# A causal convolution in front of a spectral mixer: x stored two rows to a partition, the convolution on the four quarters of the array

## The chip, the cores and the metric

The kernel runs on one core of one Trainium2 chip. The metric is device time in microseconds (us) of one execution. Three timed runs of the kernel before gave 175.7, 175.7 and 176.12 us, median 175.7 us. The core's engines have these names in the rows: PE is TensorE's matmul stream and PEld its weight loads, DVE is VectorE, ACT is ScalarE, POOL is GpSimd (here it issues the input transfers) and SP is the queue of the output transfers.

## The reference

Two blocks, one after the other, on `x` of shape (8, 3264, 192):

```python
# block 1: softmax over 7 taps for each of 8 heads, causal convolution along the rows
w = softmax(weight, axis=-1)                       # (8 heads, 7 taps)
x_pad = concatenate([zeros((B, 6, D)), x], axis=1)
u = einsum('hk,bskhg->bshg', w, x_pad[:, s + k])   # 24 columns to a head
# block 2: 64 lowest modes of the row axis are mixed over the 192 columns
X = rfft(u, axis=1)[:, :64]
Y = X @ (w_r + 1j * w_i)                           # one 192 x 192 matrix for each mode
u = u + irfft(Y, n=3264, axis=1)
out = u + relu(u @ w_ch)
```

The input x and the output are 20 MB each in float32, the mode matrices 19 MB.

## The kernel before, in words

**Stages.** The kernel goes through four stages that overlap. It loads x with a cast to bf16 on the way and convolves it; it takes the forward transform as matmuls against a table (`ftab`); it mixes the modes with matrices that stream in behind x; and it forms `u`, the clamp and the sum in a second stage that writes the output while it computes.

**Units.** Each of the four pairs of batches (`q`) is cut into units of one or two blocks of 256 rows. There are 14 units, numbered from 0 by the loop over `units`: the first pair has five small ones (`UNITS0`, four of one block and one of two), the other three have three units of two blocks each (`UNITS`). Units run from the last rows of a pair to the first. The last unit of a pair also takes the 96 rows that are left over (`rest`): units 4, 7, 10 and 13. Both batches of a pair and both halves of a batch lie beside each other in the columns of an operand, so a unit of two blocks has 8 row blocks of 24 columns for a head (192 columns) and one with rest has 10 (240 columns).

**Loading.** `load_unit` issues on POOL, for each block of 128 rows, one transfer that puts one row of x into one partition; `load_rest` brings the rows left over. Then POOL issues the mode matrices (`load_w`): sixteen groups of four modes, eight into the parts of `ct` that are still unused, four into `arena`, and the last four into `arena` again, each as soon as `mix` has read the group that lay there.

**The convolution.** `conv_pass` takes two of the eight heads. The weights of a product are 64 columns of a band matrix (`bd3`), every second column of it, so that the result comes out by parities: even rows of 256 in one half of the bank, odd rows in the other. Every product contracts over all 128 partitions and writes 64 rows of results, so two of them run beside each other, in the two column halves of the array (`tile_position=(0, 64 * half)`). For each head there are four main products and four or six corrections that bring in the rows of the block before. A pass fills a pair of banks of PSUM, and one instruction empties it back into `xall`: ACT for the passes 0, 1 and 3, DVE for pass 2. Three pairs of banks go in turn.

**Around it.** `fold` (DVE) forms sums and differences of the results of a unit, right after its last pass; `dft` multiplies them with the table, at the end of the next unit; `xtrans` turns the 64 modes of a pair. `c_bank` and `g_bank` are transposes that the second stage needs; in the loop one bank of them stands in each unit from unit 6 on, the others are put between the matmuls of the mixing stage. All engines work through their instructions in the order of the program text (`manual_schedule`), so a PE that waits holds all that stands behind.

**The mixing stage.** `mix(g)` multiplies the modes of group g, `mix_copy` and `mix_trans` bring the result into the form that the second stage reads. Its last group is the last thing that the second stage waits for.

The lines of the profile that the change and the prediction touch: L174 and L185 are the loads of x, L303 those of the mode matrices, L322 the matmuls of the convolution, L344 and L346 its casts out of PSUM on DVE and ACT, L351 the fold, L366 the forward transform, L378 and L380 `xtrans`, L389 one of its copies, L396 the copies of transposed banks on ACT, L402, L426 and L429 the transposes, L498 `mix`, L526 to L548 what follows it, L644 the matmuls of the second stage, L690 its clamp and L818 matmuls without a use that keep PE occupied.

## Time and profile before

| quantity | value |
|---|---|
| median of three runs | 175.7 us (175.7 to 176.12) |
| the profiled execution's own time | 175.52 us |
| its span, first to last instruction | 173.7 us |
| PE busy in the span | 149.5 us (86%) |
| DVE, ACT, POOL busy | 125.6, 118.8, 66.0 us |
| share of transfers in the chain that ended last | 46% |
| share of PE in that chain | 37% |
| bytes read and written in HBM | 39.62 MB, 20.45 MB |

The page divides the span into 40 slices of 4.3 us and gives for each the busy share of the engines in tenths and the rate of the transfers in GB/s, counted in the bytes that are written. A row of the groups names line, engine, operation, output and inputs, shape and number, then the busy time in us and the mean of one in ns, then the idle time of the engine before them and what ended it. A row of the timeline has start and duration in us; rows of one form that follow each other are put together (x16 is sixteen of them), and for matmuls the duration reaches to the end of the last one's latency, so the step from one start to the next is the better measure of their pace. The profiled execution takes 1.8 us more than its span, and lies 0.2 us under the median.

### The profile page before, as it was taken

How to read it: one execution, taken by the hardware profiler on the slowest of the kernel's cores; microseconds unless marked ns; L12 is line 12 of the kernel's file. 1: busy time of each engine (PE TensorE's matmuls, PEld its weight loads, DVE VectorE, ACT ScalarE, POOL GpSimd, SP SyncE). 2: the span in 40 equal slices, each digit the busy share in tenths (PEclk: the TensorE clock that was granted, in tenths of full speed). 3: DMA queues.
4: the chain of work that ended last, by engine and by line, in shares of the span. 5: the costliest groups of instructions: out<-in, count | busy, mean ns of one | idle time of the engine just before them, and what ended most of it. 6: DMA issues, size and time to landing. Idle time of an engine off the chain costs nothing.

```text
span 173.7 us, 6647 instructions
## 1 busy us (share of the span) xinstructions
PE 149.5 (86%) x2837; PEld 127.8 (74%) x2837; DVE 125.6 (72%) x246; ACT 118.8 (68%) x224; POOL 66.0 (38%) x108
## 2 busy tenths in 40 slices
PE   0044898899999999799998899999999999999980
PEld 0043797789889889577865565788999988999950
DVE  3892868476778778675545542499998999999990
ACT  6369356658686686755874654588889899898850
POOL 7977997775775584344234300420000000000000
PEclk9999999999999999999999999999999999999995
DMA  2999999999999999999999996359969999999996
GB/s 17 166 173 189 193 188 191 191 189 192 191 190 191 192 204 206 206 206 206 207 208 206 207 205 115 88 191 389 388 233 396 351 357 383 337 339 385 386 356 196
DMA packets 51650, 40.85 MB, mean 235 GB/s; under 512 B 30020, under 2 KB 51524, under 8 KB 51620
## 3 DMA queue, kind: packets, MB, share of 16 engines
q0 software_dynamic: 36400, 20.06, 83.2%
q1 hardware_dynamic: 14948, 20.16, 32.5%
q8 instruction: 22, 0.36, 0.8%
q10 hardware_dynamic: 272, 0.20, 0.3%
q14 instruction: 8, 0.07, 0.1%
HBM read 39.62 MB, written 20.45 MB: 346 GB/s over the span
## 4 chain that ended last, share of the span: by engine, by line
DMA 46%; PE 37%; POOL 9%; issue 3%; DVE 1%; POOLq 0%; DVEq 0%
DMA xall<-in_x_dram 23%; PE outleft L644 18%; DMA arena<-in_moe_w_i_dram 13%; DMA ct<-in_moe_w_i_dram 11%; PE sumright L644 8%; PE mixright L644 8%; POOL xall L174 7%; DVE xall L712 1%; PE sumright L498 1%; PE trleft L429 1%; POOL loose L270 1%; PE sumright L818 0%; PE mixright L526 0%; PE mixright L548 0%; POOL arena L303 0%
## 5 line engine op out<-in xcount | busy, mean ns | idle before, releaser
L322 PEld LDWEIGHTS <-band 128*64 128x64 bf16 x944 | 38.7, 121 | 18.3 <-ACT band L241 11.1
L644 PEld LDWEIGHTS <-ct 64*128 64x128 bf16 x624 | 41.0, 94 | 4.8 <-PE trleft L644 0.5
L322 PE MATMUL cvleft<-xall,band 128*64 128x192 bf16 (+4 forms) x640 | 30.5, 248 | 13.9 <-ACT band L241 11.1
L644 PE MATMUL outleft<-mixa,gtab 64*128 64x384 bf16 x182 | 41.9, 323 | 0.1
L174 POOL DMA_DIRECT2D xall<-in_x_dram x48 | 36.0, 760 | 10.2 <-DMA xall<-in_x_dram 8.4
L644 PEld LDWEIGHTS <-gtab 64*128 64x128 bf16 x416 | 30.9, 94 | 3.0 <-PE outleft L644 1.1
L644 PE MATMUL outleft<-wa,ct 64*128 64x192 bf16 x208 | 30.4, 243 | 0.0
L351 DVE TENSOR_TENSOR arena<-xall 128x1536 bf16<-128x1536 bf16 (+1 forms) x28 | 22.4, 840 | 8.2 <-ACT xall L346 7.8
L690 ACT ACTIVATE outleft<-outleft 128x384 f32<-128x384 f32 x53 | 24.4, 477 | 4.6 <-PE outleft L644 2.3
L346 ACT CAST xall<-cvleft 128x768 bf16<-128x768 f32 (+3 forms) x29 | 21.4, 756 | 8.8 <-PE cvleft L322 7.3
L644 PE MATMUL sumright<-mixa,gtab 64*128 64x384 bf16 x92 | 25.8, 323 | 0.0
L644 PE MATMUL mixright<-mixa,gtab 64*128 64x384 bf16 x90 | 25.8, 323 | 0.0
L644 PE MATMUL outleft<-wb,ct 64*128 64x192 bf16 x104 | 23.3, 243 | 0.0
L398 DVE COPY ct<-trleft 128x1024 bf16<-128x1024 bf16 (+1 forms) x19 | 12.4, 662 | 12.7 <-PE trleft L429 7.8
L322 PE MATMUL cvright<-xall,band 128*64 128x192 bf16 (+4 forms) x304 | 15.9, 247 | 1.6 <-DVE xall L344 1.2
L396 ACT COPY ct<-trleft 128x1024 bf16<-128x1024 bf16 x13 | 13.2, 1012 | 4.6 <-PE trleft L426 2.4
L712 DVE TENSOR_TENSOR arena<-outleft,xall 128x384 f32<-128x384 f32 x27 | 14.4, 553 | 2.5 <-PE outleft L644 2.1
L346 ACT CAST xall<-cvright 128x768 bf16<-128x768 f32 (+3 forms) x13 | 9.8, 751 | 8.4 <-PE cvright L322 6.1
L644 PE MATMUL sumright<-wa,ct 64*128 64x192 bf16 x88 | 14.2, 243 | 0.0
L644 PE MATMUL mixright<-wa,ct 64*128 64x192 bf16 x80 | 13.8, 243 | 0.0
L426 PEld LDWEIGHTS <-xall 128*128 128x128 bf16 x208 | 11.7, 98 | 2.6 <-issue 0.3
L690 ACT ACTIVATE sumright<-sumright 128x384 f32<-128x384 f32 x26 | 12.3, 477 | 1.4 <-PE sumright L644 0.3
(147 smaller groups left out, 283.2 us busy)
## 6 DMA issues: line engine op xcount, KB each, us to landing
xall<-in_x_dram POOLq DMA_DIRECT2D x48, 192.0 KB, 7.9
out_dram<-arena SPq DMA_DIRECT2D x23, 384.0 KB, 4.0
out_dram<-xall SPq DMA_DIRECT2D x13, 384.0 KB, 4.1
out_dram<-ct SPq DMA_DIRECT2D x8, 384.0 KB, 4.6
ct<-in_moe_w_r_dram POOLq DMA_DIRECT2D x8, 288.0 KB, 9.4
ct<-in_moe_w_i_dram POOLq DMA_DIRECT2D x8, 288.0 KB, 10.4
arena<-in_moe_w_r_dram POOLq DMA_DIRECT2D x8, 288.0 KB, 10.5
arena<-in_moe_w_i_dram POOLq DMA_DIRECT2D x8, 288.0 KB, 10.9
```

Source lines behind the costliest of these rows:

```text
L174: nc.gpsimd.dma_start(out=xall[:, q, t % 2, k:k + 4, :], in_=src)
L270: nc.gpsimd.affine_select(out=dst, in_=dst, compare_op=ALU.not_equal, fill=fill, base=base, pattern=pattern, channel_multiplier=1)
L322: nc.tensor.matmul(o, bd3[:, h, c0:c0 + P - 1:2], xall[:, q, t, ks:ks + n, GRP * h:GRP * h + GRP], start=(main and a == 0), stop=not main, ...
L346: nc.scalar.copy(out=dst, in_=srcv)
L351: nc.vector.tensor_tensor(out=cpm[:, r, :, 0:2 * nb, :], in0=src[:, :, :, 0, :], in1=src[:, :, :, 1, :], op=op)
L396: nc.scalar.copy(out=out, in_=in_)
L398: nc.vector.tensor_copy(out=out, in_=in_)
L426: nc.tensor.transpose(o, cv[:, blk, 0:P], ident[:])
L429: nc.tensor.transpose(o[64 * i:64 * i + 64, :], cv[:, i, P:D], ident[:], tile_position=(0, 64 * i))
L644: m = nc.tensor.matmul((Z[s % NZ] if bank is None else bank)[:, cols], l, r, start=start, stop=stop, skip_group_check=True)
L690: act = nc.scalar.activation(out=z, in_=z, func=ACT.Relu)
L712: add = nc.vector.tensor_tensor(out=o[:, :, a, :], in0=Z[s % NZ][:, 0:2 * D].rearrange("p (i d) -> p i d", i=2), in1=c_rows(q, kk)[:, a, : ...
```

## The change

`xall` now holds x two neighbouring rows to a partition. `load_unit` issues one transfer for each block of 256 rows in which a partition gets two rows that lie behind each other in HBM, and `load_rest` does the same for the rows left over. Input rows are thus split by parity as the results already were.

The convolution is written anew for that layout. The band becomes two short tables for each head (`bd4`, one for each parity of the tap), and every product contracts over 64 partitions and writes 64 rows: it uses one quarter of the array (`tile_position=(64 * src, 64 * half)`). For each head and each pair of an output parity `a` and an input parity `b` there is one step. Its lower part has two products from partitions 0 to 63 (`lower`), its upper part has two or more from partitions 64 to 127 (`higher`): the same rows, the block before, and for the first rows and the rows left over further ones of 48 columns. The upper part of a step is issued eight steps after its lower part (`LAG`), since the two row halves must not write one bank at the same time; a wait on the head's last lower product stands in front. A bank now holds one head, six single banks go in turn, and each head has its own cast: heads 4 and 6 on DVE, the others on ACT. Because the results overwrite `xall` in place and the rows left over need the last rows of the pair as they were, DVE first copies these into a new tile (`side`), once for each pair of batches.

The order of the loop changes with it: the fold of a unit stands behind the second head of the next one, the banks of transposes and `xtrans` are placed by head, and after the last unit the upper parts that are still open are issued alone (`flush`).

```diff
...
+    PW = 36
+    PB = 129
...
-    xall = sb("xall", [NQ, 2, TQ, D], BF16)
-    band = sb("band", [max(H * 2 * P, MODES // 8 * 2 * D)], BF16)
+    xall = sb("xall", [NQ, TQ, 2, D], BF16)
+    band = sb("band", [max(H * 2 * PB, MODES // 8 * 2 * D)], BF16)
...
+    bd3 = band[:, 0:H * 2 * PB].rearrange("p (h c) -> p h c", h=H)
+    bd4 = band[:, 0:H * 2 * PB].rearrange("p (h v c) -> p h v c", h=H, v=2)
...
+    packed = temp(G4 * 2 * PW, BF16)
...
+    side = temp(4 * 2 * D, BF16).rearrange("p (k t d) -> p k t d", k=4, t=2)
...
-    cz = hand_out("left", "cv", (2, 2))
+    cz = hand_out("left", "cv", (1, 1, 1, 1))
     sums = hand_out("right", "sum", (1, 1))
     stacks["sum"] = stacks.pop("right")
-    cz += hand_out("right", "cv", (2,))
+    cz += hand_out("right", "cv", (1, 1))
...
     def load_unit(q, b0, nb, rest):
-        for t in range(2 * b0, 2 * b0 + 2 * nb):
-            k = 2 + 4 * (t // 2)
-            src = bass.AP(tensor=x.tensor, offset=x.offset + (2 * q * S + P * t) * D,
-                          ap=[[D, P], [HS * D, 4], [1, D]])
-            nc.gpsimd.dma_start(out=xall[:, q, t % 2, k:k + 4, :], in_=src)
-    R0 = P - RR - 16
+        for b in range(b0, b0 + nb):
+            k = 2 + 4 * b
+            src = bass.AP(tensor=x.tensor, offset=x.offset + (2 * q * S + 2 * P * b) * D,
+                          ap=[[2 * D, P], [HS * D, 4], [1, 2 * D]])
+            nc.gpsimd.dma_start(out=xall[:, q, k:k + 4, :, :].rearrange("p k t d -> p k (t d)"), in_=src)
+    R0 = (P - RR) // 2
     def load_rest():
         for i in range(2):
-            for t in range(2):
-                off = (i * S + HS * (2 - t) - (P - R0)) * D
-                src = bass.AP(tensor=x.tensor, offset=x.offset + off,
-                              ap=[[D, P - R0], [2 * S * D, NQ], [1, D]])
-                nc.gpsimd.dma_start(out=xall[R0:P, :, t, i, :], in_=src)
+            for h in range(2):
+                src = bass.AP(tensor=x.tensor, offset=x.offset + (i * S + HS * (2 - h) - RR) * D,
+                              ap=[[2 * D, RR // 2], [2 * S * D, NQ], [1, 2 * D]])
+                nc.gpsimd.dma_start(out=xall[64 * h + R0:64 * h + 64, :, i, :, :].rearrange("p q t d -> p q (t d)"),
+                                    in_=src)
...
-                                  mask=masks[:, PW * k:PW * (k + 1)].unsqueeze(1).to_broadcast([P, G4, PW]),
+        e, v = divmod(KK - 1 - k, 2)
+        nc.vector.copy_predicated(out=pk4[:, :, v, :],
+                                  mask=masks[:, PW * e:PW * (e + 1)].unsqueeze(1).to_broadcast([P, G4, PW]),
                                   data=ta3[:, :, k:k + 1].to_broadcast([P, G4, PW]))
     for g in range(4):
...
-            dst = bd3[32 * r:32 * r + 32, G4 * g:G4 * (g + 1), 32 * r:32 * r + PW]
-            srcv = pk3[32 * g:32 * g + 32, :, :]
+            c0 = 32 * (r % 2)
+            dst = bd4[32 * r:32 * r + 32, G4 * g:G4 * (g + 1), :, c0:c0 + PW]
+            srcv = pk4[32 * g:32 * g + 32, :, :, :]
...
-    def next_pair():
+    def next_bank():
         rot[0] += 1
-        return cz[(rot[0] - 1) % 3]
-    def conv_pass(q, b0, nb, rest, h2):
-        z = next_pair()
+        return cz[(rot[0] - 1) % 6]
+    LAG = 8
+    BASE = {0: 0, -1: PB, 1: PB - 1}
+    upper = []
+    def conv_step(f):
+        f()
+        while len(upper) > LAG:
+            upper.pop(0)()
+    def flush():
+        while upper:
+            upper.pop(0)()
+    def conv_head(q, b0, nb, rest, h):
+        z = next_bank()
         nk = 4 * nb + 2 * rest
         k0 = 2 + 4 * b0 - 2 * rest
-        def put(j, a, half, main, k, n, t, ks, step=1):
-            h = 2 * h2 + j
-            c0 = a + (0 if main else P)
-            o = z[64 * half:64 * half + 64, j, GRP * nk * a:GRP * nk * (a + 1)].rearrange(
+        cols = slice(GRP * h, GRP * h + GRP)
+        last = []
+        def put(src, half, a, b, x3, k, n, shift, start=False, step=1):
+            o = z[64 * half:64 * half + 64, GRP * nk * a:GRP * nk * (a + 1)].rearrange(
                 "p (k e) -> p k e", e=GRP)[:, k - k0:k - k0 + step * (n - 1) + 1:step, :]
-            nc.tensor.matmul(o, bd3[:, h, c0:c0 + P - 1:2],
-                             xall[:, q, t, ks:ks + n, GRP * h:GRP * h + GRP],
-                             start=(main and a == 0), stop=not main, tile_position=(0, 64 * half),
-                             skip_group_check=True)
-        for j in range(2):
-            for a in range(2):
-                for half in range(2):
-                    put(j, a, half, True, k0, nk, half, k0)
-        k1 = k0 + nk
-        for j in range(2):
-            for a in range(2):
-                kb = max(2 + 4 * b0, 6)
-                if k1 > kb:
-                    put(j, a, 0, False, kb, k1 - kb, 1, kb - 4)
-                put(j, a, 1, False, 2 + 4 * b0, 4 * nb, 0, 2 + 4 * b0)
-                if b0 == 0:
-                    put(j, a, 0, False, 3, 2, 1, 0, 2)
-        dst = xall[:, q, :, k0:k1, 2 * GRP * h2:2 * GRP * h2 + 2 * GRP].rearrange(
-            "p a k (j e) -> p j a k e", j=2)
-        srcv = z[:, :, 0:2 * GRP * nk].rearrange("p j (a k e) -> p j a k e", a=2, k=nk)
-        if h2 == 2:
-            nc.vector.tensor_copy(out=dst, in_=srcv)
-        else:
-            nc.scalar.copy(out=dst, in_=srcv)
+            r = slice(64 * src, 64 * src + 64)
+            c0 = BASE[b - a] + shift
+            return nc.tensor.matmul(o, bd3[r, h, c0:c0 + 64], x3[r, :, b, cols], start=start, stop=src == 1 and b == 1,
+                                    tile_position=(64 * src, 64 * half), skip_group_check=True)
+        xq = xall[:, q, :, :, :]
+        def lower(a, b):
+            first = a == 0 and b == 0
+            k1 = 2 + 4 * b0
+            put(0, 1, a, b, xq[:, k1:k0 + nk, :, :], k1, 4 * nb, 64, first)
+            last.append(put(0, 0, a, b, xq[:, k0:k0 + nk, :, :], k0, nk, 0, first).ins.name)
+        def higher(a, b):
+            if a == 0 and b == 0:
+                nop = nc.tensor.nop()
+                tc.add_manual_dep(nop.ins, last[-1], mybir.DependencyInfo(
+                    mybir.DependencyClass.Sync, mybir.DependencyReason.DATA), reason="row tiles take turns on a bank")
+            put(1, 1, a, b, xq[:, k0:k0 + nk, :, :], k0, nk, 0)
+            kb = max(2 + 4 * b0, 6)
+            if k0 + nk > kb:
+                put(1, 0, a, b, xq[:, kb - 4:k0 + nk - 4, :, :], kb, k0 + nk - kb, 64)
+            if b0 == 0:
+                put(1, 0, a, b, xq[:, 0:2, :, :], 3, 2, 64, step=2)
+            if rest:
+                put(1, 0, a, b, side[:, 1:4:2, :, :], 0, 2, 64 - R0)
+                put(1, 1, a, b, side[:, 0:4:2, :, :], 0, 2, 64 - R0)
+            if a == 1 and b == 1:
+                dst = xall[:, q, k0:k0 + nk, :, cols].rearrange("p k a e -> p a k e")
+                srcv = z[:, 0:2 * GRP * nk].rearrange("p (a k e) -> p a k e", a=2, k=nk)
+                if h in (4, 6):
+                    nc.vector.tensor_copy(out=dst, in_=srcv)
+                else:
+                    nc.scalar.copy(out=dst, in_=srcv)
+        for a in range(2):
+            for b in range(2):
+                upper.append(lambda a=a, b=b: higher(a, b))
+                conv_step(lambda a=a, b=b: lower(a, b))
     def fold(q, b0, nb, rest):
-        src = xall[:, q, :, 2 + 4 * b0:2 + 4 * (b0 + nb), :].rearrange("p a (k h) d -> p a k h d", h=2)
+        src = xall[:, q, 2 + 4 * b0:2 + 4 * (b0 + nb), :, :].rearrange("p (k h) a d -> p k h (a d)", h=2)
         for r, op in ((0, ALU.add), (1, ALU.subtract)):
-            nc.vector.tensor_tensor(out=cpm[:, r, :, 0:2 * nb, :], in0=src[:, :, :, 0, :],
-                                    in1=src[:, :, :, 1, :], op=op)
+            nc.vector.tensor_tensor(out=cpm[:, r, 0:2 * nb, :, :].rearrange("p k a d -> p k (a d)"),
+                                    in0=src[:, :, 0, :], in1=src[:, :, 1, :], op=op)
...
     prev = None
     pend = None
     for k, u in enumerate(units):
-        conv_pass(*u, 0)
-        if k == 0:
-            table(0)
-        conv_pass(*u, 1)
-        if k == 0:
-            table(1)
-        if pend is not None:
-            xtrans(pend)
-            pend = None
-        conv_pass(*u, 2)
-        if k > len(UNITS0):
-            some([next_pair()[:, 0, :]])
-        conv_pass(*u, 3)
+        for h in range(H):
+            conv_head(*u, h)
+            if k == 0 and h in (2, 4):
+                table(h // 2 - 1)
+            if h == 1 and u[1] + u[2] == NBH:
+                nc.vector.tensor_copy(out=side[64:P, :, :, :], in_=xall[64:P, u[0], TQ - 4:TQ, :, :])
+            if h == 1 and prev is not None:
+                fold(*prev)
+                if k == 1:
+                    table(2)
+            if h == 3 and pend is not None:
+                xtrans(pend)
+                pend = None
+            if h == 5 and k > len(UNITS0):
+                some([next_bank()])
         if prev is not None:
             dft(*prev)
             if prev[3]:
                 pend = prev[0]
-        if k == len(units) - 1:
-            lt += hand_out("left", "tr", (1, 1, 1, 1))
-            trans_banks(2)
-        fold(*u)
-        if k == 0:
-            table(2)
         prev = u
+    flush()
+    lt += hand_out("left", "tr", (1, 1, 1, 1))
+    trans_banks(2)
+    fold(*prev)
     trans_banks(3)
     dft(*prev)
     for g in range(NWC + NWA):
         load_w(g)
     trans_banks(3)
-    rot[0] = 2
+    rot[0] = 4
...
```

Besides, the masks that build the band, the fold, the forward transform, `xtrans` and `c_rows` are rewritten for the new layout: four masks in place of seven, and two single banks in place of a pair for `xtrans`.

40 lines of the change are left out of this document (19 added, 21 removed).

## Prediction

> **What bounds the kernel now.** I read the page first, for the rate of the transfers and the chain that ended last.
>
> ```profile
> span 173.7 us, 6647 instructions
> ...
> PE 149.5 (86%) x2837; PEld 127.8 (74%) x2837; DVE 125.6 (72%) x246; ACT 118.8 (68%) x224; POOL 66.0 (38%) x108
> ...
> GB/s 17 166 173 189 193 188 191 191 189 192 191 190 191 192 204 206 206 206 206 207 208 206 207 205 115 88 191 389 388 233 396 351 357 383 337 339 385 386 356 196
> ...
> DMA 46%; PE 37%; POOL 9%; issue 3%; DVE 1%; POOLq 0%; DVEq 0%
> ```
>
> The rate is even from the second slice to the 24th: about 190 GB/s while x comes in, 206 while the mode matrices do, then a dip and the output at 340 to 390. The chain gives 46% to transfers, and it names those of x and of the matrices. That suggests that any gain on x is a gain in time, so I asked next how busy PE is in the same stretches.
>
> ```profile
> 30.00:40.00 10.00, 8.88 (x189) 7.93 (x187) 6.41 (x9) 5.46 (x8) 7.21 (x10) 1.00 1.59 190
> 50.00:60.00 10.00, 10.00 (x214) 9.01 (x211) 7.73 (x10) 6.75 (x9) 6.03 (x11) 1.00 1.56 190
> 70.00:80.00 10.00, 9.06 (x174) 7.29 (x175) 7.02 (x12) 5.87 (x9) 4.19 (x7) 1.00 1.21 207
> 90.00:100.00 10.00, 8.58 (x158) 5.79 (x152) 5.34 (x10) 5.69 (x11) 3.66 (x6) 1.00 1.21 207
> 150.00:160.00 10.00, 10.00 (x175) 9.44 (x171) 9.64 (x20) 8.55 (x20) 0.00 (x0) 1.00 1.01 358
> ```
>
> The columns are length, then busy time of PE, PEld, DVE, ACT and POOL, granted clock, share of the transfer engines, GB/s. From 50 to 60 us PE is busy all of the time at full clock: there are two limits side by side. Where each lets go is in the timeline of PE and in the chain of transfers.
>
> ```profile
> 35.05 1.18 PE L322 MATMUL cvleft<-xall,band 128*64 128x192 bf16 x24 [0.66 <-DMA xall<-in_x_dram]
> ...
> 51.43 8.01 DMA xall<-in_x_dram
> ...
> 59.72 7.05 DMA ct<-in_moe_w_i_dram
> ...
> 68.81 0.86 PE L366 MATMUL sumright<-arena,ftab 128*64 128x384 bf16 x8
> 70.08 0.97 PE L429 MATMUL trleft<-ident,xall 128*64 128x128 bf16 x28 [0.41 <-ACT xall L346]
> ```
>
> At 35.05 us (unit 6) PE waits for x for the last time. x is complete at 59.4, but the convolution ends only at about 69: from unit 7 on PE is behind its data, by ten microseconds at the end. Later it waits again, for the matrices:
>
> ```profile
> PE sumright L498 <- DMA arena<-in_moe_w_i_dram: 1.7, 4, 0.7
> PE sumright L366 <- DVE arena L351: 0.7, 2, 0.5
> ...
> 88.51 0.61 POOL L303 DMA_DIRECT2D arena<-in_moe_w_r_dram x1 [3.14 <-PE sumright L498]
> ```
>
> These are the waits of PE from 69 to 112 us. All that PE spares between the convolution and the last group of modes is 1.7 us on the matrices; the other waits are the chain cast, fold, transform after the last unit. The third row shows that the last four loads hang on PE in turn. So a longer convolution is covered by about 2 us and then shows in full.
>
> **The change, part by part.**
>
> *The load of x.*
>
> ```profile
> xall<-in_x_dram POOLq DMA_DIRECT2D x48, 192.0 KB, 7.9
> ...
> arena<-in_moe_w_r_dram POOLq DMA_DIRECT2D x8, 288.0 KB, 10.5
> ...
> xall<-in_x_dram POOLq DMA_DIRECT2D x4, 168.0 KB, 7.8
> ```
>
> A transfer of 192 KB is 512 packets of 384 bytes; one of the matrices is 256 of 1152. At 190 and 207 GB/s on 16 engines a packet takes 32.3 and 89.0 ns, a straight line through both gives 4.0 ns and 0.0738 ns a byte, so 60.7 ns for the new 768 bytes: an estimate of 202 GB/s. x shrinks from 10.13 to 10.03 MB (the rows left over lose 16 of 112 partitions). 53.3 us become 49.6: the transfers gain 3.7 us. POOL issues 24 in place of 48; its issues are covered by the transfers. Until unit 6, which needs 5.41 MB, the gain is 2.2 us. Against it stands what PE gets in the same stretch by the terms below: 1.0 for unit 4 (192 columns on the fullest quarter in each step, 82 ns, 2.6 us in all, against 1.6 for 144 and 96 columns on each half, twice) and six visits to another form at 0.23. I set the beginning at 0, between -2.2 and +2.4.
>
> *The products.*
>
> ```profile
> 36.46 0.85 PE L322 MATMUL cvleft<-xall,band 128*64 128x192 bf16 x16
> 37.24 0.62 PE L426 MATMUL cvleft<-ident,xall 128*128 128x128 bf16 x8
> 37.79 0.85 PE L322 MATMUL cvright<-xall,band 128*64 128x192 bf16 x16
> 38.48 0.81 PE L366 MATMUL sumright<-arena,ftab 128*64 128x384 bf16 x8
> 39.13 1.65 PE L322 MATMUL cvleft<-xall,band 128*64 128x240 bf16 x40
> ...
> 47.91 0.83 PE L322 MATMUL cvleft<-xall,band 128*64 128x192 bf16 x16
> 48.57 0.83 PE L322 MATMUL cvright<-xall,band 128*64 128x192 bf16 x16
> ...
> 52.30 0.91 PE L322 MATMUL cvleft<-xall,band 128*64 128x240 bf16 x20
> 53.00 0.94 PE L322 MATMUL cvright<-xall,band 128*64 128x240 bf16 x20
> ```
>
> Sixteen products of 192 columns take 0.66 us (47.91 to 48.57), two at once, so one takes 82 ns, 0.43 ns a column; the weight loads do not show. A head costs 0.33 us. After the change it has 16 products on four quarters, four steps of 82 ns, if four run at once: 0.33 us again. Half the area at twice the number gains nothing. No row shows quarters, but both halves of the question are there:
>
> ```profile
> 85.89 0.46 PE L498 MATMUL sumright<-ct,mixa 128*16 128x192 bf16 x12
> 86.28 0.84 PE L426 MATMUL trleft<-ident,xall 128*128 128x128 bf16 x12
> ...
> L644 PE MATMUL outleft<-mixa,gtab 64*128 64x384 bf16 x182 | 41.9, 323 | 0.1
> ```
>
> Twelve products of 192 columns take 0.39 us with what follows, less than half of 12 x 82 ns: four column tiles at once. And L644 has row halves: the window from 150 us holds 175 matmuls of 192 or 384 columns, 57 ns each, where one of 192 alone takes 82. So I take four at once; the other end, row halves in turn, is a rival.
>
> *Units with rows left over (7, 10, 13).* A head takes 0.35 us now (52.30 to 53.00 for two). Afterwards the quarter from the upper rows to the upper results has 240 columns and 48 more in each step: 288 x 0.43 = 123 ns, 0.49 us a head, 1.1 us a unit. Three units: +3.3.
>
> *Changes of form.* Between 36.46 and 37.79 stand 0.66 us of products and eight transposes of 128 columns (8 x 55 ns = 0.44), together 1.10 of 1.33 us: a visit to another form costs 0.23. Between L322 and L366, both of 128 by 64, nothing is lost (38.48, 39.13). Now the convolution is of 64 by 64, and the transform, `xtrans` and the transposes of 64 columns are not. From unit 7 on that is seven visits of the transform, two of `xtrans` and three single changes around L429: 9 x 0.23 + 3 x 0.12 = 2.4; the other end is 0, if 64 columns on both sides are enough. I take 2.4, the nearest row. The Trainium skill (TensorEngine Tiling (Array Packing), Key Properties) says that changing the tiling mode, not just the tile, drains TensorE: by that rule these visits all pay and the sum is 180.9, without it 178.5. The trace agrees where forms differ, and no run here has 64 by 64.
>
> *Lag, waits, casts.* Eight upper steps remain at the end, alone: 8 x 0.12 = +1.0. The new wait in front of a head's upper part stands before everything on PE, but what it waits for was issued five steps (0.41 us) earlier and takes 0.25: nothing for two blocks; in the one-block units, with 0.2 us for five steps, up to 0.05 us a head, in the stretch where x is late.
>
> ```profile
> L346 ACT CAST xall<-cvleft 128x768 bf16<-128x768 f32 x11 | 8.6, 802 | 3.8 <-PE cvleft L322 2.8 <-DMA xall<-in_x_dram 1.0
> ...
> L346 ACT CAST xall<-cvleft 128x384 bf16<-128x384 f32 x6 | 2.7, 474 | 1.8 <-PE cvleft L322 1.7
> ...
> L351 DVE TENSOR_TENSOR arena<-xall 128x1536 bf16<-128x1536 bf16 x15 | 13.7, 955 | 6.3 <-ACT xall L346 6.3
> ```
>
> A cast of one bank takes 474 ns, where half of a pair takes 401. Heads 0 to 3 are all on ACT: 1.90 us against 1.31 on PE, 0.59 behind, and two of six banks are held by the lag. Between 0 (the next heads and the transform let ACT catch up) and 7 x 0.59 = 4.1; I take one unit's worth, +0.6. The copy into `side` is half of a fold's tile, at most 0.96 us, on DVE behind work that PE does not wait for. The last cast is one head and not two: 0.96 becomes about 0.5, and the wait of 0.41 us at 70.08 goes; then the fold is late next. Fold, transform and `xtrans` keep their elements and columns, and three masks fewer lie ahead of unit 0, in the stretch that x paces: nothing.
>
> *Sum.* 0 + 3.3 + 2.4 + 1.0 + 0.6 = 7.3 us later at the end of the convolution. Covered: 1.7 of waits on the matrices, which come 3.7 earlier, and 0.4. The second stage is as before and shifts by 5.2. Profiled execution 175.5 + 5.2 = 180.7; it stands 0.2 under the median: 180.9 us. The transfers' 3.7 us turn into idle time between the loads that wait for PE.
>
> **The rivals.** *The transfers set the end* (faster). For it: 46% of the chain and the waits on L498. PE would have to be no later; the case decides when its extra work is under the 2.1 us of cover, and gives 175.7 - 3.7 = 172.0 in full. Against it: PE alone holds the stretch from 35 to 69, and the products cannot get shorter than their columns. The Trainium skill (DMA: Bandwidth & Descriptors, Specifications) sets the smallest transfer at line rate at 512 bytes, below which writes become read-modify-write; by it 384 bytes pay and 768 do not. The trace shows 190 against 207 GB/s, 8%; at 207 x would take 48.5 us and this rival come to 170.9.
>
> *The casts set the pace*: 4.1 in place of 0.6, 184.4. For it: ACT gets a third pair of singles; against it: PE had no idle time before L322 between 36 and 70 us with casts of 802 ns.
>
> *Row halves in turn*: steps of 164 ns, 7 units x 32 x 82 ns = 18.4 more, 199. Only the missing row speaks for it.
>
> *No difference*: no cost at the changes of form and x early by 2.2 leave 2.7 of PE time against 2.1: 176.3 or a little under.
>
> **How the numbers follow.** PE-bound as summed 0.58, casts 0.20, transfers 0.13, no difference 0.04, row halves 0.05. No change is within 0.3%, about 0.5 us, which is what the runs can tell. The range goes from 176.0 (all low ends) to 187.0 (beginning +2.4 and casts +3.5 on top): it leaves out the transfers, part of no difference and the row halves. Faster 0.13, same 0.04, slower 0.83.
>
> **What the profile after would show.** x in 49 to 50 us at 200 GB/s or more; steps of four products 82 ns apart, 0.33 us a head; heads of units with rows left over near 0.49 us; gaps of 0.1 us around L366's successor; the end of the convolution at 75 to 77 us; waits of `mix` on the matrices gone and idle time of POOL on PE grown; the stage from 110 us on unchanged and later. I am wrong if PE waits for casts in every unit, if a step takes 160 ns, or if the convolution ends before 70.

## The result, and the profile after

The changed kernel takes 209.76 us (median of four runs, 209.32 to 210.84) against 175.7 us before (four runs, 175.37 to 176.12): 1.195 times the time, 95% interval 1.189 to 1.200. I had forecast 180.9 us and a range up to 187. The direction was right, the size was wrong by 29 us.

The page of the changed kernel: span and engines, PE's busy tenths, granted clock and rate in 40 slices of 5.2 us, the queue that brings instructions, the chain that ended last, and the weight loads of the convolution.

```profile
span 207.6 us, 9073 instructions
PE 171.6 (83%) x4037; PEld 141.1 (68%) x4037; DVE 130.4 (63%) x262; ACT 124.7 (60%) x266; POOL 47.9 (23%) x84
...
PE   0248684988659697899999999999999999999990
...
PEclk9999999559975969999999999999999999999998
...
GB/s 43 197 202 202 204 203 204 203 204 202 202 207 207 207 206 176 11 6 3 3 38 105 150 5 132 192 139 79 225 360 310 284 393 357 364 357 350 391 351 206
...
q8 instruction: 31, 0.51, 1.0%
...
PE 73%; issue 10%; DVE 8%; ACT 6%; POOL 1%; DVEq 0%; ACTq 0%; POOLq 0%
...
L349 PEld LDWEIGHTS <-band 64*64 64x64 bf16 x2144 | 50.7, 127 | 37.6 <-issue 36.3
```

PE has 4037 pairs of weight load and matmul for 2837 before, 1200 more, all of them in the convolution (2144 for 944). The transfers run at 202 to 204 GB/s while x comes and 207 while the mode matrices do, as forecast. But PE's tenths change between 4 and 9 in slices 4 to 17, while x and the matrices come in (up to slice 16), and stand at 9 from the 18th on. There the transfers first rest, and later they carry the output at up to 393 GB/s. The chain has 10% "issue": time in which PE waited for nothing that the profile shows. The same by stages (length; busy time and count of PE, PEld, DVE, ACT and POOL; clock; share of the transfer engines; GB/s), first after:

```profile
12.00:82.00 70.00, 52.89 (x1548) 42.61 (x1547) 30.40 (x53) 31.08 (x70) 28.31 (x48) 0.85 1.27 204
85.00:105.00 20.00, 18.97 (x652) 15.05 (x646) 12.58 (x18) 11.51 (x24) 0.00 (x0) 1.00 0.02 5
113.00:207.00 94.00, 89.28 (x1574) 74.24 (x1570) 70.76 (x140) 69.34 (x152) 8.04 (x14) 1.00 0.85 259
```

and the kernel before:

```profile
12.00:69.00 57.00, 51.97 (x1133) 46.85 (x1131) 40.71 (x59) 38.05 (x56) 40.86 (x64) 1.00 1.53 193
80.00:173.00 93.00, 86.89 (x1514) 72.31 (x1509) 69.19 (x138) 67.93 (x149) 10.40 (x18) 0.98 0.97 282
```

The convolution ends at 105.9 us after and 69.0 before (the end of the last matmul into its banks): it is 37 us later. What follows takes 101.6 us in place of 104.7, counted to the end of the span, so the loss of 34 us lies in the convolution. Inside the convolution the same work runs at two speeds: 1548 matmuls in 70 us while transfers stream (22 a us), 652 in 20 us once they rest (33 a us). In the last stage, where the output streams, PE gets through 17 a us (1574 in 94). The waits of the changed kernel, and pieces of its chain in order of time (start, length, what):

```profile
PEld L349 <- issue: 36.3, 30, 9.2
...
ACT xall L380 <- PE cvleft L349: 30.2, 26, 3.5
...
PE cvright L349 <- issue: 12.3, 7, 2.9
```

```profile
33.61 2.87 issue
...
52.36 1.99 issue
...
58.40 1.87 issue
...
70.22 1.93 issue
...
82.02 1.97 issue
```

ACT waits for PE, not PE for ACT's casts. PE stands still some 1 to 3 us at a time, and no engine, semaphore or data transfer of the program ends these gaps. A packet of the queue q8 stands before them: this queue moved 31 packets, 0.51 MB, so 16,384 bytes each. The kernel before has 22:

```profile
q8 instruction: 22, 0.36, 0.8%
```

Per pair PE executes two instructions, 8074 after and 5674 before (the expectations and the table below count two more). That is 260 and 258 to a packet, and in the first experiment below the gaps lie exactly 256 instructions apart. So a packet is a block of 256 instructions of PE, 64 bytes each. These are the times at which the blocks start in the trace, us, up to 106 us:

```
before  21.5 27.7 33.8 40.3 46.1 52.4 59.4 65.3 71.3 78.4 84.3 90.2 97.3 105.5
after   16.6 22.5 28.4 34.3 40.2 46.1 52.0 58.1 63.9 69.8 75.8 81.7 | 85.1 88.6 92.3 96.5 100.4 104.1
```

After, blocks start 5.8 to 6.1 us apart as long as x (to 55 us) and the matrices (to 83 us) stream; then they come 3.4 to 4.2 us apart. From 20 to 85 us there are eight gaps of over 1 us between the starts of two PE instructions. Seven of them end 2.2 to 2.4 us after a block's start: 28.36 and 30.61, 34.28 and 36.48, 40.19 and 42.41, 51.96 and 54.35, 58.07 and 60.27, 69.85 and 72.15, 81.69 and 83.99. From such an end, where PE steps into a block, to the start of the next packet it takes 3.7 us while transfers stream (30.61 to 34.28, 36.48 to 40.19), and 1.15 us once they rest (83.99 to 85.14). Only this time grows under load.

Before, the blocks are 5.8 to 7.1 us apart in the same stretch, and PE steps into them 2.5 to 4.8 us after their packets start: it asked for instructions almost as fast as they come. So the first reading is: while transfers stream, PE gets 256 instructions in 5.9 us, 43.4 a us; the kernel before asked for 40 (1133 and 1131 in the 57 us of its row above), and the change asks for 2400 more.

### The profile page after: what moved, and what is told of

The parts are those of the page before. It is cut to its first block, busy times and chain, and to the rows that moved or that the text cites. A ratio compares the mean times of both kernels' runs of the same rounds, so it can differ in the third digit from the quotient of the medians.

```text
span 207.6 us, 9073 instructions
## 1 busy us (share of the span) xinstructions
PE 171.6 (83%) x4037; PEld 141.1 (68%) x4037; DVE 130.4 (63%) x262; ACT 124.7 (60%) x266; POOL 47.9 (23%) x84
## 4 chain that ended last, share of the span: by engine, by line
PE 73%; issue 10%; DVE 8%; ACT 6%; POOL 1%; DVEq 0%; ACTq 0%; POOLq 0%
PE outleft L684 15%; PE cvleft L349 14%; PE cvright L349 7%; PE sumright L684 7%; PE mixright L684 6%; PE sumright L405 6%; PE trleft L465 4%; ACT xall L380 3%; PE trleft L468 3%; PE sumright L538 3%; PE trleft L684 2%; PE cvleft L465 1%; PE mixright L566 1%; DVE arena L390 1%; DVE xall L752 1%
## 5 line engine op out<-in xcount | busy, mean ns | idle before, releaser
L349 PEld LDWEIGHTS <-band 64*64 64x64 bf16 x2144 | 50.7, 127 | 37.6 <-issue 36.3
L349 PE MATMUL cvleft<-xall,band 64*64 64x192 bf16 (+4 forms) x1260 | 56.0, 270 | 15.4 <-DVE band L250 9.2
L349 PE MATMUL cvright<-xall,band 64*64 64x192 bf16 (+4 forms) x628 | 39.9, 266 | 9.6 <-issue 9.5
L380 ACT CAST xall<-cvleft 128x384 bf16<-128x384 f32 (+3 forms) x56 | 24.3, 456 | 31.2 <-PE cvleft L349 26.6
L378 DVE CAST xall<-cvleft 128x384 bf16<-128x384 f32 (+3 forms) x19 | 9.9, 523 | 27.1 <-PE cvleft L349 20.0
L380 ACT CAST xall<-cvright 128x384 bf16<-128x384 f32 (+3 forms) x28 | 12.7, 464 | 17.1 <-PE cvright L349 13.5
L178 POOL DMA_DIRECT2D xall<-in_x_dram x24 | 18.1, 765 | 17.3 <-DMA xall<-in_x_dram 16.5
L465 PEld LDWEIGHTS <-xall 128*128 128x128 bf16 x208 | 12.5, 99 | 4.0 <-issue 1.8
L349 PE MATMUL cvleft<-arena,band 64*64 64x48 bf16 x168 | 14.5, 200 | 0.8 <-issue 0.8
```

Of the source, the lines that this page charges most:

```text
L178: nc.gpsimd.dma_start(out=xall[:, q, k:k + 4, :, :].rearrange("p k t d -> p k (t d)"), in_=src)
L349: return nc.tensor.matmul(o, bd3[r, h, c0:c0 + 64], x3[r, :, b, cols], start=start, stop=src == 1 and b == 1, tile_position=(64 * src, 64 ...
L378: nc.vector.tensor_copy(out=dst, in_=srcv)
L380: nc.scalar.copy(out=dst, in_=srcv)
L465: nc.tensor.transpose(o, cv[:, blk, 0:P], ident[:])
```

## Experiments

The theory is this supply of instructions. The rivals are the quarters themselves (row halves that do not really run together, the new wait between halves), the new load, and the casts. Each experiment was run once, beside a run of the kernel before on the same chip. That took 175.2 to 175.6 us, and 177.1 beside "One form again".

**The kernel before with more instructions.** No quarters, no new load; every product is cut into two of half the columns (1824 products for 944; the 64 narrowest stay whole).

```diff
...
+            for n0, n1 in (((0, n // 2), (n // 2, n)) if step == 1 else ((0, n),)):
+                kn = k + n0
...
-                             xall[:, q, t, ks:ks + n, GRP * h:GRP * h + GRP],
+                                 xall[:, q, t, ks + n0:ks + n1, GRP * h:GRP * h + GRP],
...
```

> The kernel before, each product of the convolution cut into two of half the columns: same columns, same two halves of the array, same loads, but 7436 rows on PE in place of 5676. Theory supply (PE gets its instructions in blocks, about 256 in 5.9 us while x or the matrices stream in, and starves above that rate): 1760 more instructions are 6.9 blocks, 41 us less what PE had in hand: 195 to 212 us, idle time of PE before weight loads that nothing in the profile ends. Theory quarters (products of 64 by 64, or two row halves on one bank, are slow in themselves): no quarters here, 96 columns take half of 192, so 176 to 179 us. Theory loads (the longer transfers hold something up): 176 to 179 us.

Measured 203.67 us, the convolution's end at 98.8 us. Its waits:

```profile
PEld L324 <- issue: 27.8, 17, 3.5
...
PE cvleft L324 <- issue: 19.4, 9, 3.4
```

The same gaps and blocks 5.1 to 6.4 us apart until 88.7 us, then 3.3 to 4.0, in a kernel with whole rows. Counted in weight loads and matmuls, PE stands still after its 1210th, 1466th, 1722nd, 1978th, 2234th, 2490th, 2746th, 3002nd, 3258th and 3514th: each time exactly 256 further on, for 0.7 to 3.6 us. So the gaps stand at the edges of the blocks, whatever the product there is. The number of instructions alone is worth 28 us, and the waits with "issue" before weight loads are 27.8.

**The new load alone.** The changed kernel's load and layout with the convolution of before put back, products over 128 rows (they multiply rows with weights that belong to other rows, so what comes out is another convolution).

> The new load and layout with the convolution of the kernel before (128 rows, two column halves, pairs of banks): the convolution multiplies the wrong rows, its time and its number of instructions (5676 rows on PE) are as before. Theory supply: the time of before or up to 3 us less, 172.5 to 176.5 us. Theory quarters: the same. Theory loads: the loss is in here, 190 us or more.

```diff
-    def conv_head(q, b0, nb, rest, h):
+    def conv_pass(q, b0, nb, rest, h2):
...
+            nc.tensor.matmul(o, bd3[:, h, c0:c0 + P - 1:2],
+                             xall[:, q, ks:ks + n, t, GRP * h:GRP * h + GRP],
...
```

Measured 175.0 us beside 175.24, the convolution's end at 69.8 us, x complete at 55.2 us. The layout costs nothing, and the earlier x is worth nothing: PE sets the pace of this stretch.

**Smaller packets.** The changed kernel with x in packets of 384 bytes, as before the change (the rows left over keep 768).

```diff
+            for t in range(2):
...
+                nc.gpsimd.dma_start(out=xall[:, q, k:k + 4, t, :], in_=src)
```

> The changed kernel, but x is loaded into the new layout by twice the transfers, 384 bytes to a packet as in the kernel before. Theory supply: the blocks of instructions still come at about 5.9 us; within 4 us of the changed kernel, 206 to 214 us. Theory quarters: the same. Theory loads: without the long packets PE does not starve while x streams: 180 to 192 us.

Measured 212.05 us, blocks 5.9 to 6.2 us apart. The interval hardly knows the size of the packets. The difference of 2.3 us to the changed kernel, in one run, is what its longer packets gain here.

**Nothing streams in the second half.** The changed kernel, the first load of the mode matrices held until the convolution's last product.

```diff
+                if g == 0:
+                    tc.add_manual_dep(load.ins, after_conv.ins.name, ...)
```

> The changed kernel, but the loads of the mode matrices are held until the last product of the convolution, so that from about 52 us (x complete) to there nothing streams. Theory supply: PE starves as in the changed kernel until 52 us and no more after that; the convolution ends at 86 to 93 us in place of 106, and the end comes at conv end + 48 + 66, about 206 us. Theory quarters: the gaps stay, the convolution ends at 104 to 108 us, the end comes at about 221 us. Theory loads: like supply, since x's transfers are over by then.

Measured 212.92 us; x is complete at 55.3 us, the convolution ends at 95.7 in place of 105.9. The two stretches of this kernel:

```profile
18.00:52.00 34.00, 23.43 (x776) 18.42 (x767) 15.50 (x28) 13.17 (x35) 11.79 (x17) 0.85 1.32 203
56.00:92.00 36.00, 35.23 (x1250) 29.11 (x1248) 23.85 (x34) 23.18 (x48) 0.00 (x0) 0.98 0.02 5
```

As soon as x is in, 1250 matmuls run in 36 us (35 a us, 23 before), and PE is busy 35.2 of them. The blocks go from 5.9 us apart to 3.4 to 4.3 at that moment. This ties the slow supply to the transfers and not to the part of the program. That the end is not better is the price of the late matrices, which the mixing stage now waits for. The convolution ended three to ten microseconds later than I had said for this theory (86 to 93), and the time is 7 us above the 206.

**Fewer instructions, same columns.** Even rows from even rows and odd from odd use the same weights; the two products become one of twice the columns, 12 main products a head for 16. (`LAG` goes from 8 steps to 6, which is two heads as before.)

```diff
+            o = z[64 * half:64 * half + 64, 0:2 * GRP * nk].rearrange(
+                "p (a k e) -> p a k e", a=2, e=GRP)[:, :, k - k0:k - k0 + step * (n - 1) + 1:step, :]
+            x4 = x3[r, :, :, cols].rearrange("p k b e -> p b k e")
...
-        for a in range(2):
-            for b in range(2):
+        for a, b in ((0, 0), (0, 1), (1, 0)):
```

> The changed kernel with the two products of a step that use the same weights (even rows from even, odd from odd) put into one of twice the columns: 12 main products of a head for 16, the same columns in all. PE's rows fall from 8076 to 7004. Theory (PE waits for its instructions, which come at 43.4 rows a us while x and the weights stream, up to about 83 us, and at about 68 a us after it): the convolution has 2230 rows in the kernel before, 3560 here; 43.4 x (83 - 11) = 3125 of them by 83 us and the other 435 in 6.4 us, so its end at about 89.5 us (after 105.8) and the time at about 193 us (186 to 198). Rival (the quarters themselves, or the switching between row halves, cost the time): as many columns, as many changes of half: 203 to 209 us.

Measured 197.76 us, the convolution's end at 94.7 us. Twelve microseconds gained by the number alone, with all the quarters and changes of half in place. The theory had 193 (186 to 198) and the convolution's end at 89.5. The rate held while transfers streamed (blocks 6.0 us apart on average from 26.6 to 80.9 us); my count of the beginning and of the quick phase was too kind.

**And without the narrow products**: the merged kernel with the sums over the block before the first one and over the rest's neighbours left out.

```diff
-            if b0 == 0:
-                put(1, 0, a, b, xq[:, 0:2, :, :], 3, 2, 64, step=2)
-            if rest:
-                put(1, 0, a, b, side[:, 1:4:2, :, :], 0, 2, 64 - R0)
-                put(1, 1, a, b, side[:, 0:4:2, :, :], 0, 2, 64 - R0)
```

> The merged kernel (197.8 us) without the products that fetch the block before the first one and the rest's neighbours (their sums are left out of the result): PE's rows 6428 for 7004, the wide products all there. By the instruction supply: 2980 rows of the convolution; the merged kernel ended it at 94.7 us with 3560, in phases with 43 rows a us: 13 us less, so the convolution's end at 81 to 84 us and 183 to 189 us. By the columns alone (the 288 narrow products had 48 or 96 columns, at most 41 ns each): 12 us less at most if they are on the path one by one, 6 us if they go in pairs: 186 to 192.

Measured 189.38 us, the convolution's end at 85.5 us. This lies just above what I gave for the supply and inside what I gave for the columns: as a test it does not tell the two apart. It tells something about the granted clock.

```profile
PEclk9999999999999999999999999999999999999995
```

In the changed kernel three slices stand at half clock, one at 0.6 and one at 0.7; in the merged one a single slice stands at 0.6. Here none falls while x and the matrices come in, and the blocks are 6.0 to 6.3 us apart all the same. So the low clock is not what spaces the blocks.

**The kernel before with only its main products cut.**

```diff
+            for n0, n1 in (((0, n // 2), (n // 2, n)) if main else ((0, n),)):
```

> The kernel before with the main products alone cut into halves of their columns (the neighbours' stay whole): PE's rows 6572 for 5676, no quarters, every product over 128 rows, the same columns. By the instruction supply: 3126 rows of the convolution at 43.4 a us from 11 us on, its end at 83 us, 14 after the kernel before: 189 us (183 to 194). By what a product costs beside its columns (bounded by the cut of all products, 203.7 us, of which half): 189 as well, but then evenly, without gaps of 2 us and more; without any cost of number: 175 to 177.

Measured 187.9 us, the convolution's end at 82.0 us (83 expected), and not evenly:

```profile
PEld L324 <- issue: 17.4, 12, 3.2
...
PE cvleft L324 <- issue: 9.3, 6, 3.1
```

Both ideas gave about this time, but only the supply gave standstills of 2 us and more: an even cost of each product is not what is seen.

**Whole columns where it can be.** In the merged kernel, output rows 64 to 127 take from all 128 input rows; if the band of the upper rows is stored 64 columns further on, one product of 128 rows serves in place of two quarters, 9 main products a head.

```diff
-    PB = 129
+    PB = 193
...
-            c0 = 32 * (r % 2)
+            c0 = 32 * r
...
-            put(0, 1, a, b, xq[:, k1:k0 + nk, :, :], k1, 4 * nb, 64, first)
+            put(2, 1, a, b, xq[:, k1:k0 + nk, :, :], k1, 4 * nb, 64, first)
```

> The merged kernel, and of the four quarters the two that write output rows 64 to 127 become one product over all 128 input rows (the upper rows' band is stored 64 columns further on, so that one column range serves both halves): 9 main products of a head. PE's rows 6524. Theory of the instruction supply: 3080 rows of the convolution at 43.4 a us from 11 us on: its end at about 82 us, 13 after the kernel before, and the time at about 187 us (180 to 192). Rival (quarters or changes of half): the changes of half on the other output half remain, as many as before: over 197 us.

Measured 302.06 us. Neither theory had that. PE's timeline of this kernel:

```profile
59.96 0.67 PE L355 MATMUL cvleft<-xall,band 128*64 128x192 bf16 x2
60.26 0.37 PE L355 MATMUL cvright<-xall,band 64*64 64x192 bf16 x1
60.56 0.98 PE L355 MATMUL cvleft<-xall,band 128*64 128x384 bf16 x2
61.02 0.52 PE L355 MATMUL cvright<-xall,band 64*64 64x384 bf16 x1
```

Products over 128 rows and over 64 alternate. (A row x2 holds a 128-row product and the 64-row one behind it, which also writes `cvleft`; the two 64-row products of a step start together.) Each form starts 0.30 us after the other where 192 columns take 82 ns, and 0.46 us after it where 384 take 164. So the two forms do not overlap, and a change of form costs 0.22 to 0.30 us here. (Blocks of instructions come 10 to 25 us apart during most of it: here nobody waits for them.)

**One form again**: the same kernel, the product over 128 rows cut to its upper 64; what the lower input rows add to the upper output rows is left out.

```diff
-            put(2, 1, a, b, xq[:, k1:k0 + nk, :, :], k1, 4 * nb, 64, first)
+            put(1, 1, a, b, xq[:, k1:k0 + nk, :, :], k1, 4 * nb, 64, first)
```

> The kernel with whole columns (302 us), its product over 128 input rows cut to the upper 64: the same number of products, the same columns, banks, weights' table and order, and every conv product again of 64 rows by 64 columns. It leaves out what the lower input rows add to the upper output rows. If the changes between products over 128 rows and over 64 cost the time (each step of 192 columns took 300 ns there in place of 82): gone, PE's rows are 6524, which by the instruction supply gives a convolution that ends at 82 to 87 us and 186 to 192 us. If something else of that kernel costs it (the wider table, the number or the order of the products): 280 us and more.

Measured 191.07 us, the convolution's end at 87.9 us (82 to 87 expected); the steps are 80 ns apart again (rows start at 59.95 and 60.03 in place of 60.26 and 60.56).

```profile
59.95 0.24 PE L355 MATMUL cvright<-xall,band 64*64 64x192 bf16 x2
...
60.03 0.25 PE L355 MATMUL cvright<-xall,band 64*64 64x192 bf16 x2
```

Number, columns, banks, table and order of the products are the same in both, so the 111 us are the price of alternating the two forms.

**What in the transfers delays the blocks?** First the number of transfers of x under way at a time (n = 2, then 1):

```diff
+            if len(loads) >= n:
+                tc.add_manual_dep(load.ins, loads[-n], ...)
+            loads.append(load.ins.name)
```

> The changed kernel, each of the 24 transfers of x waits until the second before it has landed. If the blocks of instructions come late because they stand behind queued data packets, the interval of 5.9 us between two blocks falls (to 3.5 to 5 us) while x is loaded, the gaps of 2 to 3 us on PE get fewer, and the time falls below the 209.8 us to 190 to 204, though x lands later than at 52 us. If the interval is set by the share of bandwidth alone, or by PE's own fetching, it stays at 5.9 us in this phase and the time is 207 to 214 us.

> As with two, but each transfer of x waits for the one before it, so that a queue of x's packets can never stand for longer than one transfer. Queue theory: blocks on demand, 3.4 to 4.5 us apart, no gap of PE that ends after a block's start while x is loaded, but x lands at 80 to 100 us and may now set the convolution's end (about 90 to 105 us), so 190 to 212 us. Rival: 5.9 us apart as before, 209 us or more.

Measured 213.71 us with two and 248.49 us with one (the convolution's end at 110.8 and 145.6 us; x complete at 74.4 and 128.4 us). With one, x comes in at 64 to 107 GB/s in nearly all slices, and PE then waits for x itself; where PE is not waiting for x the blocks are mostly still 4.6 to 5.6 us apart (71.7, 76.3, 81.5; 102.1, 107.4, 112.5), once 3.5. With two they are 4.7 to 7.7 us apart while x comes in, once 3.3. Thinner traffic shortens the interval a little at best and is no remedy. The theory that the blocks stand behind a long queue of x's packets missed both times as I put it. It is not excluded: with one transfer under way the next packet starts 0 to 3.1 us after PE's step into a block, where the changed kernel had 3.7.

Then the kind of queue: SP issues the transfers into x's buffer, as it does for the output, and the matrices are held as above. What it moves is one block of constants, so this kernel does not convolve x.

```diff
-            nc.gpsimd.dma_start(out=xall[:, q, k:k + 4, :, :].rearrange("p k t d -> p k (t d)"), in_=src)
+            nc.sync.dma_start(out=xall[:, q, k:k + 4, :, :].rearrange("p k t d -> p k (t d)"), in_=xhalf[:, :, :].rearrange("k p d -> p k d"))
```

> The changed kernel with the mode matrices held until the convolution is done, and the 24 transfers into x's buffer issued by SP, from one block of bf16 constants in DRAM, in place of POOL's transfers that read x and convert it: the same bytes written in the same packets of 768 bytes, but half the bytes read and a queue described by hardware. It computes the convolution of constants, not of x. If only the converting queue of POOL delays the blocks of instructions: blocks 3.3 to 4.6 us apart from the start, no gap over 1 us on PE once the first data are there, the convolution's end at 80 to 87 us (after the kernel with the same held matrices had it at 95.7) and 197 to 205 us. If any transfer that streams delays them: 5.3 us and more while x comes, gaps of 2 us and more there, the convolution's end at 88 us or later and 206 to 213 us.

Measured 206.78 us, the convolution's end at 89.5 us. Its two stretches:

```profile
18.00:37.00 19.00, 14.42 (x492) 11.40 (x482) 11.54 (x23) 8.41 (x24) 0.00 (x0) 1.00 1.05 352
40.00:85.00 45.00, 43.53 (x1541) 35.29 (x1540) 29.78 (x44) 28.66 (x61) 0.00 (x0) 0.99 0.02 5
```

At 352 GB/s, through another queue, the blocks are 5.3 to 5.5 us apart until x is complete at 37.8 us, and 3.4 to 4.5 after it: 26 matmuls a us, then 34. So it is not the converting queue of POOL alone: loads by another queue slow the supply as well.

The runs side by side, by PE's instructions. Left out are the runs with something else changed: small packets, held matrices, forms in alternation, throttled x, and constants by SP.

```
                       PE's instructions   convolution's end   time
before                       5676               69.0           175.7
new load alone               5676               69.8           175.0
no narrow products           6428               85.5           189.4
main products cut            6572               82.0           187.9
one form                     6524               87.9           191.1
merged                       7004               94.7           197.8
all products cut             7436               98.8           203.7
the change                   8076              105.9           209.8
```

Against the kernel before, each thousand instructions more costs 14 to 18 us, whether the products are quarters or whole rows.

## Why the prediction was wrong

**The beginning and the load: right.** x was to come at 202 GB/s and 3.7 us earlier than 59.4 us; it came at 202 to 204 and was complete at 55.3. That this gain would be hidden behind PE was right too (the new load alone: 175.0).

**The products: their time right, their number wrong.** Once nothing streams, four products on four quarters start 82 ns apart, as I took it:

```profile
89.20 0.25 PE L349 MATMUL cvright<-xall,band 64*64 64x192 bf16 x2
89.25 0.27 PE L349 MATMUL cvleft<-xall,band 64*64 64x192 bf16 x2
89.28 0.24 PE L349 MATMUL cvright<-xall,band 64*64 64x192 bf16 x2
```

(The next step begins at 89.28, after 89.20.) The step that failed is the sentence "Half the area at twice the number gains nothing": I weighed the gain of it and not its price. The number of instructions was no term of my sum: 2400 more were priced at nothing, and their supply accounts for 22.5 to 25 of the 29 to 31 us by which the convolution ended later than forecast (worked out below). I saw "the weight loads do not show" and took it that instructions do not cost; I did not ask how PE comes by them. The traces of before had hints of it: a queue named "instruction" with 22 packets of 16 KB, their spacing of 5.8 to 7.1 us in just the stretch that I called PE-bound, and 5.5 us of "issue" before weight loads of L322 in the waits list.

The sum that I left out can be made from the traces of both. PE has 2304 instructions up to the convolution's end before, 4704 with the change's 2400. At 43.4 a us from 9 us, where PE starts, to 83, where the matrices end, it gets through 3212; the other 1492 take 23 us at the 65 a us of the quick phase (652 and 646 in 20 us): 106 us, as measured. Only the closest spacing of the blocks, 5.8 us, could be read before; that it was a limit, and the quick rate, could not.

What the supply accounts for: at 33 matmuls a us, as from 85 to 105 us, the 1548 matmuls of the stretch from 12 to 82 would have taken 47.5 us and not 70, 22.5 less; by the 35 a us of the run with held matrices, 25. The convolution ended at 105.9, and 75 to 77 was forecast, 29 to 31 less. Four to nine microseconds are thus not accounted for by this, and their cause stays open. The edges of blocks in the quick phase are not it: in the run with held matrices PE stands still at most 0.23 us at an edge from 56 to 92 us.

**Units with rows left over: nearly right.** From 98.78 to 101.70 us 143 matmuls of the last unit take 2.92 us, 20.4 ns each; with 28 to a head that is 0.57 us, where I had 0.49: 0.6 us more for a unit of eight heads.

**Changes of form: right in size.** A visit of the transform takes 0.77 us for eight matmuls of 384 columns, two at once (98.01 to 98.78): 8 x 164 / 2 = 0.66 and 0.11 more. The last step before it starts at 97.83, so 0.18 us pass in place of 0.08: another 0.10 going in. Together that is 0.21, where I took 0.23. Where forms alternate at every step it is 0.22 to 0.30 for each change, by the run with whole columns. The rule of the Trainium skill that I leaned on (TensorEngine Tiling (Array Packing), Key Properties: a change of the tiling mode drains TensorE) agrees with both.

**Casts, lag, waits: right that they are small.** ACT and DVE waited for PE. The waits of `mix` on the matrices went, as said; PE comes so late that POOL then waits 32.5 us for it before it can load into `arena`.

**The rivals.** The transfers do not set the end, and the casts do not set the pace. The row halves do run together; that rival's 199 us came nearest by accident. A rival "PE runs out of instructions" was missing.

The Trainium skill (Runtime: NRT & Kernel Launch, Instruction fetch mechanics) says that an engine's sequencer fetches its instructions in blocks of 16 KiB, 256 of them, by a DMA queue of its own. These traces agree: 16,384 bytes to a packet, gaps 256 instructions apart. The same section of the Trainium skill says that the cost of crossing a block is mostly hidden. These traces contradict it while transfers stream: 1 to 3 us at a crossing in the changed kernel. By that rule the change would have cost nothing for its number, and my 180.9 would have stood; the measurement decides.

## What to carry to other kernels

Count the instructions that an engine gets, not only its busy time: on PE each matmul with new weights is two, and in this kernel 256 of them came in 5.9 us while transfers streamed. A tiling that makes products smaller and more numerous has to be held against that rate in the stretch where the loads run; the spacing of the instruction queue's packets in the trace says how near the limit a kernel already is. And keep products of one form together: alternating 128 and 64 rows cost 0.22 to 0.30 us a change.

## What the runs showed of the hardware that was not expected

When PE uses up its instructions fast, blocks of 256 start 5.1 to 6.5 us apart in the convolution while x or the matrices stream in at about 180 to 370 GB/s, by POOL's or by SP's queue, in packets of 384, 768 or 1152 bytes. (One came after 3.7 us, at 58.4 us in the run with only the main products cut.) When nothing streams they start 3.3 to 4.6 us apart. A block is usable 2.2 to 2.6 us after its packet starts, under load or not; what grows is the time before the packet starts, from about 1 us to 3.7.

The output does not do this: from 157 to 189 us of the changed kernel it streams at 284 to 393 GB/s, and the next packet starts 0.5 to 1.7 us after PE's step into a block. What in the loads makes this time longer was not found. Packet size and the kind of queue change it little, and fewer transfers under way shorten it only in part.

In the changed kernel the granted clock falls to half three times, for about 20 us in all (35.8 to 46.1, 59.7 to 66.6, 73.4 to 76.8 us; mean 0.85 from 12 to 82 us). Each fall comes in or within 1.3 us after a gap of 1.9 us or more, but two such gaps have no fall behind them. The blocks come no faster at full clock (52.0 to 58.1) than at half (40.2 to 46.1).

And 128-row and 64-row products do not overlap when they alternate: 302 us for a kernel that takes 191 in one form.
